# Token mixes beside the first chunks, and channel mixes at the full height of the array

## The chip, the cores and the metric

The kernel runs on one core of a Trainium2 chip. The metric is the device time of one execution in microseconds (us). The engines are called TensorE (PE in the profile; PEld is its weight load), VectorE (DVE), ScalarE (ACT), GpSimd (POOL) and SyncE (SP, which here only issues DMAs); a q behind a name is the engine's sequencer. In this kernel matmuls write to banks of PSUM, and all other tiles on the chip lie in SBUF. The record marks each run as fast or slow; all runs quoted are fast.

## The reference, cut to what matters

```python
# x: 8 x 4224 x 192, weight: 8 heads x 7 taps
w   = softmax(weight)                                  # per head
x   = causal 7-tap convolution of x along seq with w   # "conv"
theta = x @ w_theta                                    # 192 x 192, a channel mix
zr, zi = x * cos(theta), x * sin(theta)
y   = einsum('ts,bsd->btd', w_tok_r, zr) + einsum('ts,bsd->btd', w_tok_i, zi)   # 4224 x 4224 each
u   = x + y
out = u + relu(u @ w_ch)                               # a second channel mix
```

The token mixes are nearly all of the arithmetic: 33 row blocks of 128 tokens, 33 chunks of 128 source tokens, two matrices, and 1536 columns (batch times channel) in three PSUM banks of 512. That is 33 x 33 x 2 x 3 = 6534 matmuls of 128x512.

## The kernel before

The 33 chunks are handled in three passes of 11. In a pass, every row block is mixed with the pass's 11 chunks; part sums go to DRAM between the passes. The chunks of the next pass are prepared beside the mixes of this one. Only the first 11 chunks have no such company: the start has to make them while nothing, or little, can be mixed.

```python
def channel_mix(dst, tT, w):            # 192 channels = 128 + 64 rows of the array
    R = D - P                           # 64
    for q in range(2):
        v = [dst[k][:, q * D : (q + 1) * D] for k in range(2)]
        for k in range(2):              # two matmuls on all 128 rows
            pe(nc.tensor.matmul(v[k], lhsT=tT[:, 3 * q + 2 * k, :], rhs=w[:, 2 * k, :],
                                start=True, stop=False))
        for k in range(2):              # two on 64 rows each, upper and lower half
            pe(nc.tensor.matmul(v[k], lhsT=tT[k * R : (k + 1) * R, 3 * q + 1, :],
                                rhs=w[k * R : (k + 1) * R, 1, :], start=False, stop=True))

# class Chunk ... (cut)
    # conv(hp): matmuls into a PSUM bank, then ScalarE copies it to xz (two buffers);
    #           when xz is whole, four DMAs write it to the scratch xs in DRAM
    # transpose(g), theta(g): six PE transposes; channel mix; clamp on VectorE; two Sin on ScalarE
    # times_x(): z *= x on VectorE, 128x768, one for zr and one for zi

# the start: 5 PSUM banks for mixes, 3 for the rest
    y0 = [bank("y", "y") for _ in range(NP)]        # row block 0, three column blocks
    y1 = [bank("y", "y") for _ in range(2)]         # row block 1, two of three
    for i in range(nc0 + 3):
        # ... weights and chunk loads cut
        for half in range(2):
            if old: old.theta(half)                 # chunk i - 1
            next(m, 0)                              # one of five mixes per step
            if ch:
                ch.conv(2 * half); ch.conv(2 * half + 1)    # chunk i
            if old: old.times_x()
            next(m, 0)
        # ...
        for half in range(2):
            if ch: ch.transpose(half)
            next(m, 0)
```

## Time and profile before

1673.58 us, median of 4 runs (1673.18 to 1674.23).

The page of the kernel before: busy time of the engines, and the chain of work that ended last, by engine and then by line.

```profile
PE 1618.1 (97%) x8738; PEld 759.3 (45%) x8910; DVE 870.9 (52%) x1550; ACT 231.0 (14%) x366; POOL 509.7 (31%) x948
PE 93%; issue 1%; ACT 1%; DVE 1%; DMA 1%; SPq 0%; DVEq 0%; ACTq 0%
```

TensorE is the limit, but "97% busy" doesn't say how densely it works. The timeline does. These are lines of the third pass (start, length, engine, operation, count); ends overlap, so read the starts.

```profile
1294.24 0.38 PE L331 MATMUL y<-zr,wt_10762 128*128 128x512 bf16 x1
1294.46 0.38 PE L331 MATMUL y<-zi,wt_10828 128*128 128x512 bf16 x1
1294.67 0.33 PE L276 MATMUL v<-wch,uT 128*128 128x192 bf16 x2
1294.93 0.26 PE L281 MATMUL v<-wch,uT 64*128 64x192 bf16 x2
1295.12 0.34 PE L276 MATMUL v<-wch,uT 128*128 128x192 bf16 x2
1295.39 0.26 PE L281 MATMUL v<-wch,uT 64*128 64x192 bf16 x2
```

A mix starts every 0.2157 us. Two full-height channel matmuls start 82 to 94 ns apart (in the records of single instructions), two half-height ones 3 ns apart, that is, together; but each change of height takes 179 to 186 ns. All eight take 0.91 us. In the same way six transposes take 0.335 us and eight conv matmuls 0.55.

From these paces comes the measure used below. For each of TensorE's weight loads, of which no record is missing, add up what all matmuls issued before it take at the dense pace (idle matmuls, which the change adds, count as nothing). The clock minus that sum is what TensorE has **lost so far**. Before, the dense sum is 6534 x 0.2157 + 132 x 0.335 + 66 x 0.55 + 132 x 0.91 = 1610 us; of the span of 1671.0 us, 61.0 are lost: 12.2 when the first conv starts, 52.2 by 150 us, and only 8.8 in all the rest.

What it waited for (the waits view of the kernel before: who, for whom, us in total, times, longest; "..." marks lines left out, here and below):

```profile
PE pc L202 <- DMA xw<-in_x_dram: 12.2, 1, 12.2
PE th L276 <- ACT xz L209: 10.5, 6, 3.1
...
PE y L331 <- DVE wt_327 L319: 3.1, 1, 3.1
```

and one such wait in the chain of the kernel before (start, length, what):

```profile
57.51 3.02 DMA xs<-xz
60.52 0.01 issue
60.53 0.83 ACT zi L245
61.36 0.38 ACT xz L209
61.74 0.04 issue
61.78 0.24 PE th L276
```

The chain names the DMA that writes xz to scratch, and the prediction took from it that ScalarE's next copy waits for this DMA, since xz has two buffers. ScalarE's two longest sums in the waits view (to 130 us), and its timeline:

```profile
ACT xz L209 <- PE pc L202: 33.1, 15, 8.3
ACT zr L242 <- DVE ang L237: 23.5, 10, 4.9
```

```profile
59.69 0.94 ACT L242 ACTIVATE zr<-ang,half_pi 128x768 bf16<-128x768 f32 x1 [1.91 <-DVE ang L237]
60.53 0.83 ACT L245 ACTIVATE zi<-ang 128x768 bf16<-128x768 f32 x1
61.27 0.85 ACT L209 ACTIVATE xz<-pc 128x384 bf16<-128x384 f32 x2
```

The DMA in the chain writes the *other* buffer of xz. The one that the copy at 61.27 fills had been written to scratch by 53.83 us; for chunks 2 to 10 that write landed at least 4.3 us before the copy. What the copy stands behind is ScalarE's own pair of Sin (zr, zi), which waited for VectorE's clamp; in all six of TensorE's waits of this kind the copy follows the pair without a gap. So the buffers of xz are not what held the chunks here; ScalarE's order is.

The sums by stretch of the kernel before (window, its length, then busy us and count of PE, PEld, DVE, ACT and POOL, granted clock, DMA share, which passes 1 where the packets' times overlap, GB/s):

```profile
20.00:60.00 40.00, 30.16 (x202) 14.03 (x206) 26.56 (x52) 19.72 (x33) 21.28 (x39) 0.91 0.98 150
60.00:100.00 40.00, 31.40 (x268) 14.91 (x271) 26.02 (x52) 26.51 (x44) 13.76 (x24) 1.00 0.91 148
```

The clock of 0.91 leaves something out: the trace's first clock record is at 40.3 us, and until then matmuls run at half pace (transposes start 106 to 107 ns apart, and 56 later; mixes about 400 ns, and 216 later).

### The profile page before, as it was taken

Reading aid. Unit: us, or ns where it says so; the run is one execution under the profiler, and the core shown is the slowest. Engines: PE = TensorE matmul, PEld = TensorE weight load, DVE = VectorE, ACT = ScalarE, POOL = GpSimd, SP = SyncE. Lnnn points to the kernel's source line nnn. Section 1 sums busy time; section 2 is a strip of 40 time slices with the busy share of each in tenths; the row PEclk is TensorE's granted clock in tenths of the full one; section 3 lists DMA queues with packets and bytes.
Section 4 is the critical chain, followed back from the end, with each engine's and each line's share of the span. In section 5 each row is a group of like instructions: output and inputs, shape, how many; then the busy total and the mean of one; then the engine's idle time right before and its main releaser. Section 6 shows DMA issues by size and latency. Waiting matters only on the chain.

```text
span 1671.0 us, 22525 instructions
## 1 busy us (share of the span) xinstructions
PE 1618.1 (97%) x8738; PEld 759.3 (45%) x8910; DVE 870.9 (52%) x1550; ACT 231.0 (14%) x366; POOL 509.7 (31%) x948
## 2 busy tenths in 40 slices
PE   4889999999999999999999999999999999999998
PEld 2334444444444444444444444444444444444444
DVE  5664444444444434444444444446666666666664
ACT  3640111111111001111111111101111111111111
POOL 6523333333333333333332332232222222222220
PEclk9999999999999999999999999999999999999999
DMA  9957665656566677777777776776766676667661
GB/s 145 153 109 134 126 128 108 129 120 113 119 120 107 144 175 174 164 178 161 164 177 170 161 180 166 160 172 150 169 153 165 157 162 162 160 163 163 160 160 64
DMA packets 221291, 248.36 MB, mean 149 GB/s; under 512 B 58752, under 2 KB 193920, under 8 KB 221184
## 3 DMA queue, kind: packets, MB, share of 16 engines
q0 software_dynamic: 152256, 85.24, 41.7%
q1 hardware_dynamic: 68928, 161.67, 27.0%
q8 instruction: 70, 1.15, 0.3%
q14 instruction: 37, 0.30, 0.1%
HBM read 235.27 MB, written 90.83 MB: 195 GB/s over the span
## 4 chain that ended last, share of the span: by engine, by line
PE 93%; issue 1%; ACT 1%; DVE 1%; DMA 1%; SPq 0%; DVEq 0%; ACTq 0%
PE y L331 84%; PE tp L260 2%; PE v L276 2%; PE v L281 1%; PE th L276 1%; PE pc L202 1%; PE th L281 1%; DMA xs<-xz 1%; ACT xz L209 0%; ACT zi L245 0%; DVE ang L237 0%; DVE uT L264 0%; SPq L220 0%; DVE zi L251 0%; DVE pv L362 0%
## 5 line engine op out<-in xcount | busy, mean ns | idle before, releaser
L305 POOL DMA_DIRECT2D st<-in_moe_w_tok_i_dram x396 | 212.7, 544 | 682.0 <-DVE wt_1340 L319 29.6
L305 POOL DMA_DIRECT2D st<-in_moe_w_tok_r_dram x396 | 212.7, 544 | 363.4 <-issue 18.1
L364 DVE TENSOR_TENSOR pv<-y,pv 128x512 f32<-128x512 f32 x198 | 136.6, 690 | 258.6 <-PE y L331 249.3
L362 DVE COPY pv<-y 128x512 f32<-128x512 f32 x99 | 68.2, 690 | 198.8 <-PE y L331 195.3
L264 DVE COPY uT<-tp 128x768 bf16<-128x768 bf16 x132 | 73.4, 557 | 170.0 <-PE tp L260 169.6
L242 ACT ACTIVATE zr<-ang,half_pi 128x768 bf16<-128x768 f32 x66 | 61.7, 935 | 623.6 <-DVE ang L237 623.5
L368 ACT ACTIVATE ub<-pv 128x512 bf16<-128x512 f32 x99 | 62.3, 629 | 517.4 <-DVE pv L364 517.4
L237 DVE TENSOR_SCALAR ang<-th 128x384 f32<-128x384 f32 x132 | 67.5, 551 | 78.9 <-PE th L281 78.9
L386 DVE SCALAR_TENSOR_TENSOR pv<-v,pv 128x384 f32<-128x384 f32 x132 | 67.5, 553 | 75.3 <-PE v L281 75.3
L209 ACT ACTIVATE xz<-pc 128x384 bf16<-128x384 f32 x132 | 57.7, 487 | 285.0 <-PE pc L202 169.2
L187 POOL DMA_DIRECT2D xw<-in_x_dram x132 | 76.7, 592 | 66.4 <-PE pc L202 55.3
L354 DVE TENSOR_TENSOR pv<-pv,xr 128x512 f32<-128x512 f32 x99 | 66.3, 670 | 0.0
L276 PEld LDWEIGHTS <-uT 128*128 128x128 bf16 x528 | 40.2, 98 | 43.8 <-DVE uT L264 2.1
L276 PE MATMUL th<-wth,uT 128*128 128x192 bf16 x264 | 47.2, 259 | 10.7 <-ACT xz L209 10.5
L245 ACT ACTIVATE zi<-ang 128x768 bf16<-128x768 f32 x66 | 54.7, 829 | 0.0
L202 PE MATMUL pc<-xw,bands 96*64 96x192 bf16 x528 | 38.5, 264 | 15.2 <-DMA xw<-in_x_dram 12.2
L281 PEld LDWEIGHTS <-uT 64*128 64x128 bf16 x528 | 25.4, 93 | 54.9 <-issue 54.9
L276 PE MATMUL v<-wch,uT 128*128 128x192 bf16 x264 | 44.1, 249 | 0.7 <-DVE uT L264 0.7
L202 PEld LDWEIGHTS <-bands 96*64 96x64 bf16 x528 | 22.2, 113 | 44.5 <-issue 31.4
L251 DVE TENSOR_TENSOR zr<-xz,zr 128x768 bf16<-128x768 bf16 x66 | 35.0, 530 | 9.1 <-ACT zr L242 9.0
L260 PE MATMUL tp<-ident,xz 128*128 128x128 bf16 x396 | 37.5, 233 | 2.1 <-ACT xz L209 1.8
L260 PEld LDWEIGHTS <-xz 128*128 128x128 bf16 x396 | 29.6, 105 | 21.0 <-ACT xz L209 8.3
(629 smaller groups left out, 3612.4 us busy)
## 6 DMA issues: line engine op xcount, KB each, us to landing
st<-in_moe_w_tok_r_dram POOLq DMA_DIRECT2D x396, 88.0 KB, 3.3
st<-in_moe_w_tok_i_dram POOLq DMA_DIRECT2D x396, 88.0 KB, 3.3
part_83<-pv SPq DMA_DIRECT2D x33, 768.0 KB, 3.9
pv<-part_83 SPq DMA_DIRECT2D x33, 768.0 KB, 4.3
part_84<-pv SPq DMA_DIRECT2D x33, 768.0 KB, 3.8
pv<-part_84 SPq DMA_DIRECT2D x33, 768.0 KB, 5.0
out_dram<-pv SPq DMA_DIRECT2D x66, 384.0 KB, 4.0
xs<-xz SPq DMA_DIRECT2D x132, 96.0 KB, 3.7
```

What stands on the lines that cost most here:

```text
L187: nc.gpsimd.dma_start(out=self.xw[lo : lo + n, h, :, :], in_=x[:, t0 : t0 + n, :].rearrange("b s d -> s b d"),)
L202: pe(nc.tensor.matmul(pc[half * 2 * Q : (half + 1) * 2 * Q, hh * B * G : (hh + 1) * B * G], lhsT=bands[:, h, :, :].rearrange("p a m -> p ( ...
L237: dve(nc.vector.tensor_scalar(out=every_other(ang[:, :, :], k), in0=pair(th[k]), scalar1=-CLAMP, scalar2=CLAMP, op0=ALU.max, op1=ALU.min,))
L260: pe(nc.tensor.transpose(tp[:, k * P : (k + 1) * P], u[:, k * P : (k + 1) * P], ident))
L264: dve(nc.vector.tensor_copy(out=uT[:, :, :].rearrange("p k s -> p (k s)"), in_=tp[:, 0 : 6 * P]))
L276: pe(nc.tensor.matmul(v[k], lhsT=tT[:, 3 * q + 2 * k, :], rhs=w[:, 2 * k, :], start=True, stop=False,))
L305: nc.gpsimd.dma_start(out=st[a * Q : (a + 1) * Q, :, 0 : self.ncs * Q], in_=w[self.tb * P : (self.tb + 1) * P, t0 : t0 + self.ncs * Q] .re ...
L331: pe(nc.tensor.matmul(y, lhsT=w.wt[m][:, c, :, :].rearrange("p bt i -> p (bt i)"), rhs=zs[c][m][:, cols], start=(c == 0 and m == 0), stop= ...
L354: dve(nc.vector.tensor_tensor(out=self.pv[:, cols], in0=self.pv[:, cols], in1=self.xr[:, cols], op=ALU.add,))
L362: dve(nc.vector.tensor_copy(out=pj, in_=y))
L364: dve(nc.vector.tensor_tensor(out=pj, in0=y, in1=pj, op=ALU.add))
L386: dve(nc.vector.scalar_tensor_tensor(out=pk, in0=pair(v[k]), scalar=0.0, in1=pk, op0=ALU.max, op1=ALU.add,))
```

## The change

The intent: fill TensorE's waits in the start with the mixes of four row blocks instead of five thirds; take the height changes out of the channel mixes, by padding the 64-row weights with zeros to 128 rows. The diff, cut to its core (... marks cuts; the comments sum up what is cut):

```diff
-        t = constp.tile([P, 3, D], BF16, name=name)
+        t = constp.tile([P, 4, D], BF16, name=name)
+        nc.vector.memset(t[:, 1:3, :], 0.0)
 ...
-            channel_mix(th, self.xT[g], wth)     # full, full, half, half
+    def channel_mix(tT, k, w):
+        v = bank("mm", "v")
+        for b in range(2):
+            for i in range(2):
                 pe(nc.tensor.matmul(
+                    v[:, b * D : (b + 1) * D], lhsT=tT[:, 3 * k + b + i, :],
+                    rhs=w[:, 2 * b + i, :], start=(i == 0), stop=(i == 1),
                 ))
 ...
-                self.xz = wk.tile([P, B, D], BF16, name="xz", tag="xz")
+                self.xz = wk.tile([P, B, D], BF16, name="xz",
+                    tag="xw" if early[0] and self.c % 2 else "xz")
 ...
+    def times_x(self, g):                      # one step later than before
+            for z in (self.zr, self.zi): ...
+                if early[0] and z is self.zi and g == 0:
+                    nc.gpsimd.tensor_tensor(**args)
+                else:
+                    dve(nc.vector.tensor_tensor(**args))
 ...
+    class Piece:                               # one column block of one row block: 12 of them
+        def leave(self):                       # its PSUM bank is wanted
+            self.give(True)
+            if self.part is None:              # first part sum: ScalarE copies it to SBUF
+                tag = ("zr", "zi")[len(parts) % 2]     # a buffer of the next pass's chunks
+                self.part = zpool.tile([P, PC], F32, name="part", tag=tag)
+                act(nc.scalar.activation(out=self.part, in_=self.y, func=AT.Copy))
+            else:                              # later ones: VectorE adds
+                dve(nc.vector.tensor_tensor(
+                    out=self.part, in0=self.y, in1=self.part, op=ALU.add))
+        ...
+        def fill(ready, n):                    # mix n pairs (one chunk, one piece)
+            for k in range(n):
+                held = [o for o in pieces if o.y is not None]
+                can = [o for o in held if o.can(ready)]
+                new = [o for o in pieces if o.y is None and o.can(ready)]
+                if not can and new:
+                    if len(held) == 4:
+                        max(held, key=lambda o: o.c).leave()
+                    can = new
+                if not can:
+                    return n - k
+                can[0].take()
+            return 0
 ...
+        pinned[0] = True                       # VectorE's (and ScalarE's) order is fixed from here on
+        idle(12)                               # matmuls on zeros, for the clock
+        for i in range(nc0 + 2): ...
+            # conv 0 1, two pairs, theta 0 (chunk i-1), products (chunk i-2), two pairs,
+            # conv 2 3, a weight transpose, two pairs, theta 1, four Sin, two pairs,
+            # then twice: transpose, weight transpose, one pair.
+            # Where there is no pair yet and i < 5, an idle matmul.
```

The first x load is also issued before the masks are made, and the conv bands are built from one block instead of two.

## The prediction

> **What bounds the kernel.** TensorE. The page gives PE 97% of the 1671.0 us span and the chain of waits puts 93% on PE, 84% on the token mixes. In the timeline a mix matmul (128x512) follows the last every 0.2157 us, a group of six transposes takes 0.335, eight conv matmuls 0.55, eight channel-mix matmuls 0.91. Times the counts (6534 mixes, 132 transpose groups, 66 conv groups, 132 channel mixes) this is 1409.7 + 44.2 + 36.3 + 120.1 = 1610 us, an estimate from these durations. So 61 us of the span are not dense TensorE work: comparing running sum and clock, 12.2 us before the first conv (which waits for the first x load), about 40 us between 12 and 120 us, 2.2 us from 120 to 1666, and 6.6 us in the tail. The waits view names the middle part: TensorE's theta matmuls wait for ScalarE's conv evictions, and the chain goes back to the scratch write of xz (3.0 to 4.3 us each), since xz has only two buffers; chunks then come every 7 to 8 us and only five mixes share that time.
>
> **Change 1, full-height channel mixes.** The timeline of single instructions shows two full-height 128x192 matmuls starting 82 ns apart, two 64-row ones 3 ns apart (concurrent), but 179 to 186 ns at each switch between the heights, with the next weight load held back. The Trainium skill, "TensorEngine Tiling (Array Packing)", Key Properties, says that a mode switch drains TensorE; the trace agrees, about 100 ns beyond the 82. Eight full-height matmuls should need 8 x 0.082 = 0.66 us: 0.25 saved in each of 132, 33 us, of which 110 (28 us) lie in dense TensorE time, so on the critical path. Zero padding doubles those rows' arithmetic and costs nothing else.
>
> **Change 2, the start.** Four row blocks (132 mix pairs, 57 us) are mixed beside the first chunks instead of five thirds (24 us). Odd chunks' xz take other buffers, bands cost less DVE, the first x load is issued before the masks, and idle matmuls keep the clock up. Counting the new order with the durations above: 3.9 to 5.7 us for each of the first five steps, up to 7.4 for the later ones, 19 us of mixes left after the last: 112 us at best for 91 us of work, 21 lost. DVE gets 6 to 7 us per step, ScalarE 5 to 6; part sums add 12 ScalarE copies and some 20 DVE adds of about 0.65 us, hidden. The DMA engines, busy above 90% until 90 us already, get two more row blocks of weights; by their packet times a step with a chunk and half a row block needs near 8 us. I expect 24 to 35 us lost instead of 52, so about 24 saved.
>
> **Sum.** Dense 1577 + start 28 + drip 2 + tail 7 + hand-over 2 = 1616 us; 8 in 10: 1603 to 1634. Faster by over 2% 0.94, within 2% 0.05, slower 0.01.
>
> **What would show it.** The channel mix: starts 82 ns apart, one form 128*128, a pass-2 row block about 0.5 us shorter. The start: chunk steps of 7 to 8.5 us, the first conv near 11 us, no theta waiting on xz, the wait for DMA larger; mixes dense by 115 to 125 us.
>
> **What would make it wrong.** GpSimd, which now also does one product per chunk, stuck behind DMA issues that wait for buffers; VectorE over 8 us per step because evictions and weight transposes queue in fixed order; three PSUM banks for conv, theta and transposes stalling TensorE: 10 us a step would cost 20 more. If full-height matmuls of alternating weights take 0.1 us each, 19 us of change 1 vanish.

## The result, and the profile after

1632.28 us, median of 4 runs (1626.16 to 1636.74), against 1673.58. The ratio is 0.975, 95% interval 0.9718 to 0.9782, so faster. The prediction said 1616, with 1603 to 1634: the measured time lies inside, but just, and one of the four runs lies outside. Note the spread: 10.6 us over four runs, against 1.1 before.

The page of the kernel after:

```profile
PE 1599.9 (98%) x8962; PEld 793.8 (49%) x8962; DVE 879.6 (54%) x1543; ACT 238.1 (15%) x379; POOL 527.7 (32%) x961
PE 95%; DMA 2%; POOL 1%; DVE 1%; issue 0%; ACT 0%; SPq 0%; DVEq 0%; POOLq 0%
```

The timeline of the kernel after: a channel mix of the third pass is now one line, of one form.

```profile
1265.68 0.82 PE L243 MATMUL v<-wch,uT 128*128 128x192 bf16 x8
```

With 0.66 us for eight (the starts of the eight are 82 to 83 ns apart; the 0.82 includes the last one's end), the dense sum becomes 1577 us. From 150 us to the last weight load the kernel then loses only 2.9 us, so that pace is right. The channel mix is worth what was promised. The start isn't: TensorE has lost 45.3 us by 150 us, 6.9 less than before, where 28 were expected in the start and 2 at the hand-over to the next stage. The waits view of the kernel after:

```profile
PE y L290 <- DVE part L425: 7.7, 3, 5.1
PE spare L549 <- POOL ident masks.py:199: 6.7, 1, 6.7
PE tp L229 <- DVE ang L198: 6.5, 4, 3.6
```

ScalarE's xz is gone from it. VectorE stands in its place, with single waits of 3.6 and 5.1 us. (The line of "spare" is the idle matmuls waiting for their operand, before the first conv.) The stretches of the kernel after:

```profile
20.00:60.00 40.00, 33.83 (x298) 20.07 (x296) 35.98 (x60) 27.15 (x45) 33.71 (x51) 1.00 1.19 201
60.00:100.00 40.00, 33.06 (x245) 19.02 (x245) 33.33 (x57) 20.62 (x34) 19.88 (x28) 0.87 0.65 98
```

VectorE is busy 36 and 33 of 40 us: it has hardly any slack left. The granted clock is 0.87 in the second stretch, where the kernel before had 1.00. The wait of 3.6 us costs more than itself: TensorE loses 3.9 us in it, and 2.75 more from 61.6 to 67.7 us, while the granted clock is 0.5 (0.66 in the slice from 60 to 70 us).

The wait of 3.6 us in the timeline of the kernel after:

```profile
54.80 3.15 DVE L223 TENSOR_TENSOR zr<-xz,zr 128x768 bf16<-128x768 bf16 x2
...
55.40 1.65 POOL L221 TENSOR_TENSOR zi<-xz,zi 128x768 bf16<-128x768 bf16 x1
...
57.87 1.98 DVE L223 TENSOR_TENSOR zi<-xz,zi 128x768 bf16<-128x768 bf16 x1
...
59.33 2.01 POOL L221 TENSOR_TENSOR zi<-xz,zi 128x768 bf16<-128x768 bf16 x1
59.77 0.68 DVE L425 TENSOR_TENSOR part<-y,part 128x512 f32<-128x512 f32 x1
60.37 0.70 DVE L276 STREAM_TRANSPOSE wt<-st 128x512 bf16<-128x512 bf16 x1
61.00 0.98 DVE L198 TENSOR_SCALAR ang<-v 128x384 f32<-128x384 f32 x2
...
61.56 0.80 PE L229 MATMUL tp<-ident,xz 128*128 128x128 bf16 x6 [3.62 <-DVE ang L198]
```

A product on VectorE takes 0.55 us elsewhere. Here two together take 3.15 and one takes 1.98, each time with a product of GpSimd near. Behind them, in VectorE's fixed order, stand an addition of a part sum and a weight transpose, and only then the clamp that frees the PSUM bank TensorE needs. Six of VectorE's products are long like this, 9.7 us in excess of 0.55 each; the kernel before has none. A third wait, of 2.3 us before 107.11, has no long product in it: VectorE is doing clamps, three products of 0.55 us and three additions there.

### The profile page after: what moved, and what is told of

Read it like the earlier page. It is cut to its first block, busy times and chain, and to the rows that moved or that the text cites. A ratio compares the mean times of both kernels' runs of the same rounds, so it can differ in the third digit from the quotient of the medians. Undisturbed runs are those within 1.5% of the kernel's fastest.

```text
span 1630.4 us, 22878 instructions
## 1 busy us (share of the span) xinstructions
PE 1599.9 (98%) x8962; PEld 793.8 (49%) x8962; DVE 879.6 (54%) x1543; ACT 238.1 (15%) x379; POOL 527.7 (32%) x961
## 4 chain that ended last, share of the span: by engine, by line
PE 95%; DMA 2%; POOL 1%; DVE 1%; issue 0%; ACT 0%; SPq 0%; DVEq 0%; POOLq 0%
PE y L290 86%; PE v L243 5%; PE tp L229 3%; PE pc L165 1%; DMA xw<-in_x_dram 1%; POOL xw L147 1%; DMA st<-in_moe_w_tok_i_dram 1%; DVE zi L223 0%; DMA xw<-xw 0%; DVE zr L223 0%; POOL st L262 0%; DVE part L425 0%; POOL zi L221 0%; DVE ang L198 0%; DVE wt L276 0%
## 5 line engine op out<-in xcount | busy, mean ns | idle before, releaser
L290 PE MATMUL y<-zr,wt 128*128 128x512 bf16 x3267 | 1240.4, 380 | 8.4 <-DVE part L425 7.7
L290 PE MATMUL y<-zi,wt 128*128 128x512 bf16 x3267 | 1239.8, 379 | 0.0
L290 PEld LDWEIGHTS <-wt 128*128 128x128 bf16 x6534 | 628.5, 98 | 718.0 <-issue 11.7
L276 DVE STREAM_TRANSPOSE wt<-st 128x512 bf16<-128x512 bf16 (+1 forms) x594 | 366.8, 645 | 0.0
L321 DVE COPY pv<-y 128x512 f32<-128x512 f32 x87 | 60.1, 690 | 201.8 <-PE y L290 186.0
L243 PEld LDWEIGHTS <-uT 128*128 128x128 bf16 x1056 | 92.1, 99 | 34.3 <-issue 3.1
L198 DVE TENSOR_SCALAR ang<-v 128x384 f32<-128x384 f32 x132 | 67.3, 549 | 50.7 <-PE v L243 44.4
L243 PE MATMUL v<-wth,uT 128*128 128x192 bf16 x528 | 56.4, 250 | 1.1 <-DVE uT L233 0.9
L243 PE MATMUL v<-wch,uT 128*128 128x192 bf16 x528 | 54.4, 246 | 0.7 <-DVE uT L233 0.7
L229 PE MATMUL tp<-ident,xz 128*128 128x128 bf16 x396 | 33.2, 220 | 6.6 <-DVE ang L198 6.5
```

The lines of the kernel that those rows point to most:

```text
L198: dve(nc.vector.tensor_scalar(out=af[:, k * 2 * D : (k + 1) * 2 * D], in0=channel_mix(self.xT[g], k, wth), scalar1=-CLAMP, scalar2=CLAMP, ...
L229: pe(nc.tensor.transpose(tp[:, k * P : (k + 1) * P], u[:, k * P : (k + 1) * P], ident))
L243: pe(nc.tensor.matmul(v[:, b * D : (b + 1) * D], lhsT=tT[:, 3 * k + b + i, :], rhs=w[:, 2 * b + i, :], start=(i == 0), stop=(i == 1),))
L276: dve(nc.vector.transpose(self.wt[m][:, c:ce, :, :], self.st[m][:, :, c * Q : ce * Q].rearrange("p bt (c j) -> p c bt j", j=Q),))
L290: pe(nc.tensor.matmul(y, lhsT=w.wt[m][:, c, :, :].rearrange("p bt i -> p (bt i)"), rhs=zs[c][m][:, cols], start=(c == first and m == 0), s ...
```

## The experiments

Three theories for the 15 us or so by which the start falls short (45.3 lost against 28 and 2):

- **Theory 1**: GpSimd's product and VectorE's products exclude each other. The Trainium skill, "SBUF — State Buffer", section "SBUF: two separate sides", says that VectorE's second port pair is shared with GpSimd under "an exclusive lock, not a bandwidth split", for a VectorE operation with two SBUF inputs against a GpSimd operation that reads SBUF.
- **Theory 2**: VectorE simply has too much to do, in a fixed order: 22 additions of part sums, weight transposes, clamps.
- **Theory 3**: GpSimd's queue. Its product stands behind weight loads, which wait for staging buffers.

| run | us, median | TensorE's loss by 150 us | long products on VectorE, excess us |
|---|---|---|---|
| before | 1673.6 | 52.2 | 0 |
| after | 1632.3 | 45.3 | 6, 9.7 |
| e1, only the full-height channel mixes | 1645.5 | 59.0 | 0 |
| e2, after, all products on VectorE | 1623.9 | 34.9 | 0 |
| e3, after, two products on GpSimd | 1627.4 | 39.5 | 8, 11.2 |
| e4, after, least mixed piece first | 1618.1 | 31.1 | 4, 6.8 |
| e6, after, four staging buffers | 1624.4 | 38.7 | 2, 2.7 |
| e5, e2 and e4 together | 1614.9 | 27.9 | 0 |
| e7, e5 without idle matmuls | 1614.9 | 27.8 | 0 |
| e8, e5 with two xz buffers | 1645.7 | 58.9 | 0 |
| e9, e5 with two row blocks | 1627.2 | 39.4 | 0 |
| e10, e7 with four side banks | 1618.9 | 31.2 | 0 |
| e11, e5 and a useless GpSimd product | 1625.0 | 39.7 | 10, 15.0 |
| e12, e5 and GpSimd memsets | 1615.1 | 29.0 | 0 |

"Long" is over 0.7 us; the last two columns come from each run's trace, the last from its single instructions. All results were correct. The runs are from five sets of rounds; the kernel before took 1673.6 to 1674.0 us in each, so they can be compared.

**e1: the channel mixes alone.** In the kernel before, with the weights padded as in the change (not shown):

```diff
-        for q in range(2):
-            # full, full, half, half
+        for k in range(2):
+            for q in range(2):
+                for i in range(2):
+                    pe(nc.tensor.matmul(dst[k][:, q * D : (q + 1) * D],
+                        lhsT=tT[:, 3 * q + k + i, :], rhs=w[:, 2 * k + i, :],
+                        start=(i == 0), stop=(i == 1)))
```

> The kernel before with only the full-height channel mixes (same loop of chunks, same buffers). From the durations: 132 channel mixes go from 0.91 to 0.66 us, 33 us in all, of which the 110 after the start (28 us) lie in dense TensorE time and the 22 of the start are partly hidden behind waits. Expected 1643 to 1648 us. If the start's rearrangement were what paid, this would give under 15 us.

1645.45 us, against 1673.92 in the same rounds: 28.5 us. The dense sum falls by 33, and the start gives 6.8 back (59.0 lost instead of 52.2), because there TensorE only waits longer. The rest of the change is therefore worth 1645.5 - 1632.3 = 13.2 us, not the 24 (plus those few) that I had put on it.

**e2: no product on GpSimd.**

```diff
-                if early[0] and z is self.zi and g == 0:
-                    nc.gpsimd.tensor_tensor(**args)
-                else:
-                    dve(nc.vector.tensor_tensor(**args))
+                dve(nc.vector.tensor_tensor(**args))
```

> The kernel after with all four products of a chunk on VectorE, none on GpSimd. Theory 1 (the GpSimd product and VectorE's two-input products exclude each other: VectorE products of 1.2 to 2.7 us where GpSimd's is near, 0.55 elsewhere): no VectorE product over 0.7 us, TensorE's waits of 3.6 and 5.1 us in the start gone, 1617 to 1625 us. Theory 2 (VectorE has too much work in fixed order: evictions of part sums, weight transposes): 11 more products of 0.55 us, so the same time or up to 6 us slower. Theory 3 (GpSimd's queue: the product waits behind weight loads that wait for staging buffers): also faster, as theory 1.

1623.94 us, 8.3 less, though VectorE has 11 products more; no product is long. Theory 2 alone would have made it no faster. Theories 1 and 3 stand.

**e3: two products on GpSimd.**

```diff
-                if early[0] and z is self.zi and g == 0:
+                if early[0] and z is self.zi:
```

> The kernel after with both zi products of a chunk on GpSimd (two instead of one). Theory 1: more meetings, more VectorE products over 1 us (10 or more against 6), the time longer by 5 us or more. Theory 2: VectorE has 6 us less work in the start, so faster by some us.

1627.43 us (1626.16 to 1628.84): not slower, and by the medians 4.9 faster, though the runs of the two overlap. The long products were 8 and their excess 11.2 us, only 1.5 more than after, while VectorE was spared 11 products, 6 us. Theory 1's forecast of the time failed, and theory 2 has a share. It looks as if VectorE's time as a whole is what is short, whether it goes into products, into being held, or into additions.

**e4: fewer additions.** The list of pieces that can be mixed is in the order of row blocks, so the early ones come back for one chunk each time, and each visit costs an addition.

```diff
-                    can = new
+                    can = [min(new, key=lambda o: o.c)]
```

> The kernel after, but a free PSUM bank goes to the piece with the fewest chunks mixed, instead of the first in the list: by counting the order, 10 VectorE additions of part sums instead of 22, 2 instead of 17 of them before the last chunk. GpSimd's product is kept. Theory 2: 10 us of VectorE work out of the start, the waits of TensorE for VectorE mostly gone, about 10 us faster. Theory 1: the long products stay, and only the waits for additions go: 2 to 5 us faster.

1618.05 us (1615.56 to 1624.95), 14.2 less: more than either forecast. VectorE has 10 additions instead of 22 (6.6 us instead of 14.6). Four long products are left, with 6.8 us in excess instead of 9.7, so the gain is not from the additions alone.

**e5: both cures.**

> All products on VectorE and, for a free bank, the piece with the fewest chunks mixed. If the two costs (long products beside GpSimd's, 22 part-sum additions on VectorE) are separate, TensorE loses about 28 us by 150 us from the start, against 45.3 in the kernel after, 34.9 without the GpSimd product and 31.1 with the other order alone: 1611 to 1616 us. If they are one and the same slack, no better than 1617.

1614.87 us (1614.79 to 1615.40 in five runs). The loss by 150 us is 27.9, as expected; the spread has shrunk to 0.6 us. The two cures overlap: 8.3 and 14.2 us apart, 17.4 together. The stretches of this run:

```profile
20.00:60.00 40.00, 36.55 (x326) 21.95 (x325) 36.94 (x74) 29.36 (x49) 26.79 (x49) 1.00 1.24 208
60.00:100.00 40.00, 40.00 (x305) 22.61 (x303) 28.57 (x58) 26.20 (x42) 15.72 (x28) 1.00 0.89 148
```

From 60 to 100 us TensorE is busy without a break at full clock, with VectorE at 28.6 of 40. From 20 to 60 VectorE is still busy 36.9 of 40 us.

**e6: GpSimd's queue.**

```diff
-            st = wpool.tile([P, NQ, NCMAX * Q], BF16, name="st", tag="st", bufs=3)
+            st = wpool.tile([P, NQ, NCMAX * Q], BF16, name="st", tag="st", bufs=4)
```

> The kernel after with four staging buffers for raw token weights instead of three, so that GpSimd's queue, in which the product stands behind weight loads, no longer waits for a VectorE transpose. Theory 3 (the queue makes the product late): the waits of 3.6 and 5.1 us go, 1620 to 1625 us. Theories 1 and 2: the products still meet, VectorE still does the additions; 1628 to 1636 us.

1624.43 us, 7.9 less: what theory 3 expected. But the trace shows how: with an earlier queue the products meet less often (2 long ones, 2.7 us excess). The queue sets *when* GpSimd's product runs; e6 doesn't say what the meeting itself costs. For that, e11 and e12.

**e11 and e12: the meeting by itself.** All results come from VectorE, as in e5. GpSimd does something useless when VectorE's first product of a step is done:

```diff
                 dve(nc.vector.tensor_tensor(**args))
+                if early[0] and z is self.zi and g == 0:
+                    # e11
+                    nc.gpsimd.tensor_tensor(out=scratch[0], in0=self.xf[:, cols],
+                                            in1=self.zr[:, cols], op=ALU.mult)
+                    # e12, in its place
+                    nc.gpsimd.tensor_copy(out=scratch[0][:, 0:8],
+                                          in_=self.zr[:, cols.start : cols.start + 8])
+                    nc.gpsimd.memset(scratch[0], 0.0)
+                    nc.gpsimd.memset(scratch[0], 1.0)
```

> Both cures, all results from VectorE, and in each step one useless GpSimd product of the same size (128x768, two inputs in SBUF) that starts when VectorE's first product is done, its result never read. Theory 1: VectorE's products right after it last 1.2 us or more in most of the 11 steps, with no other change of VectorE's work; 3 to 10 us slower than the 1614.9 without it. If the long products came from something else in the kernel after (order, queue): all products stay at 0.55 us and the time within 1 us.

> The same with two GpSimd memsets of that tile behind an 8-element copy, instead of the product: GpSimd is busy at the same place, but hardly reads SBUF. Theory 1 in the form that a read port is shared (the Trainium skill's page on SBUF says so): VectorE's products stay at 0.55 us, the time within 1 us of 1614.9. If any GpSimd work beside VectorE costs: long products here too.

e11 took 1624.98 us (1620.61 to 1626.50), 10.1 more than e5; e12 took 1615.05, 0.2 more. The groups of e11 from 0 to 112 us (busy us, mean ns of one):

```profile
L221 DVE TENSOR_TENSOR zr<-xz,zr 128x768 bf16<-128x768 bf16 x22 | 23.9, 1087 | 0.1
...
L223 POOL TENSOR_TENSOR scratch<-xz,zr 128x768 bf16<-128x768 bf16 x11 | 19.0, 1729 | 19.6 <-DVE zr L221 19.6
...
L221 DVE TENSOR_TENSOR zi<-xz,zi 128x768 bf16<-128x768 bf16 x22 | 15.2, 692 | 0.0
```

and the same groups of e12:

```profile
L221 DVE TENSOR_TENSOR zi<-xz,zi 128x768 bf16<-128x768 bf16 x22 | 12.1, 549 | 0.2 <-ACT zi L213 0.2
L221 DVE TENSOR_TENSOR zr<-xz,zr 128x768 bf16<-128x768 bf16 x22 | 12.1, 548 | 0.1
...
L227 POOL MEMSET scratch<- 128x768 bf16 x11 | 8.4, 759 | 0.0
```

One of the 11 meetings in the timeline of e11:

```profile
50.23 0.55 DVE L221 TENSOR_TENSOR zi<-xz,zi 128x768 bf16<-128x768 bf16 x1
...
50.48 1.79 POOL L223 TENSOR_TENSOR scratch<-xz,zr 128x768 bf16<-128x768 bf16 x1 [4.36 <-DVE zr L221]
50.69 1.99 DVE L221 TENSOR_TENSOR zr<-xz,zr 128x768 bf16<-128x768 bf16 x1
...
52.61 0.55 DVE L221 TENSOR_TENSOR zi<-xz,zi 128x768 bf16<-128x768 bf16 x1
```

GpSimd's product begins at 50.48 and ends at 52.27. VectorE's, begun at 50.69, ends at 52.68: 0.4 us after it, as if it had waited for the whole of it; all ten long ones end 0.41 to 0.43 us after the GpSimd product beside them. Their excess is 15.0 us in all. A GpSimd that is as busy (19.9 us against 19.0), but hardly reads, changes nothing: in e12 the records of single instructions have six memsets that overlap a product, by 0.14 to 0.55 us, and those products take 0.545 to 0.557 us. Nor is it GpSimd's issuing of DMAs: in e5, 32 of the 44 products overlap an issue, and none takes more than 0.56 us. That a GpSimd product with SBUF inputs blocks VectorE's two-input product is shown; that the read port is what they share is the skill's account, and e12 agrees with it, as far as its short overlaps go.

**e7: the idle matmuls.**

```diff
-        idle(12)
-                if i < 5:
-                    idle(few)
```

> The run with both cures, without the idle matmuls (12 before the first conv, about 40 in the first five steps). If they keep the granted clock up: some stretches at half clock before 50 us, 2 to 6 us slower than with them. If they only stand in the way of the real matmuls: 1 to 4 us faster.

1614.91 us against 1614.87: no difference. The granted clock is 0.72 and 0.76 in the slices from 20 to 30 and from 30 to 40 us, 1.00 with the idle matmuls; TensorE isn't the limit there, so nothing is lost by it.

**e8: two buffers of xz.**

```diff
-                    tag="xw" if early[0] and self.c % 2 else "xz",
+                    tag="xz",
```

> The run with both cures, but every chunk's xz in the same two buffers, as in the kernel before. If the scratch write of xz was what held the chunks up before: ScalarE's copies wait for it again in most steps from the fourth on, up to 1.5 us each, 4 to 10 us slower. If the longer steps (7.4 us of TensorE work against 5) hide the write: within 2 us.

1645.66 us (1644.63 to 1652.12), 30.8 more; the largest effect of all, and not for the reason I gave. The timeline of e8:

```profile
81.14 0.55 DVE L220 TENSOR_TENSOR zr<-xz,zr 128x768 bf16<-128x768 bf16 x1
81.61 0.55 DVE L220 TENSOR_TENSOR zi<-xz,zi 128x768 bf16<-128x768 bf16 x1
...
82.24 1.64 ACT L172 ACTIVATE xz<-pc 128x384 bf16<-128x384 f32 x4 [4.96 <-issue]
82.78 0.36 PE L165 MATMUL pc<-xw,bands 96*64 96x192 bf16 x4 [1.94 <-ACT xz L172]
```

The last product that reads the old xz ends at 82.16, and ScalarE's copy into that buffer starts 0.08 us later; for each of chunks 2 to 10 it is 0.08 to 0.16 us. It isn't the DMA to scratch that holds the buffer in this order, it is the products: the change does them one step later than before, so it *needs* more buffers of xz. The scratch write of the old xz had landed at least 6.5 us before each of these copies, so it would not have held them.

**e9: two row blocks.**

```diff
-    EARLY = 4
+    EARLY = 2
```

> The run with both cures, with two row blocks mixed beside the first chunks instead of four. Of 57 us of early mixes 28.5 are left. If the number of row blocks fills the waits of the later steps: TensorE runs dry in steps 6 to 12, 8 to 16 us slower than with four (1623 to 1631 us). If the other parts of the change (more xz buffers, orders) already keep the steps short, since a step then needs only about 6 us: within 4 us.

1627.17 us, 12.3 more, in the expected range. Up to 80 us the loss is almost that of e5 (29.8 against 26.9); after it TensorE runs dry (37.8 against 26.8 at 100 us). The four row blocks earn their keep in the second half of the start.

**e10: the bank of the idle matmuls.**

```diff
-        open_psum(stack, 5, 3)
+        open_psum(stack, 4, 4)
```

> Both cures, no idle matmuls, and the PSUM bank that those used given to conv, theta and transposes: four banks for them, four for mixes. In the first five steps TensorE's transposes wait 0.76 us in each of two steps for a clamp to free one of three banks. If those three banks set the pace of the early steps (6.9 us each, for 3.1 us of work): 2 to 5 us faster, 1610 to 1613. If ScalarE's and VectorE's chain of fixed order does: the same within 1 us.

1618.91 us, 4.0 more than e7, which neither reading expected. By 40 us the loss is lower (23.3 against 24.6), so the three banks seem to cost a little (one trace of each); but the waits of this run show what the fifth mix bank was for:

```profile
PE y L287 <- ACT part L420: 3.7, 5, 0.9
PE y L287 <- DVE part L422: 2.1, 3, 0.9
```

Four pieces are held at most, and the fifth bank lets the next begin while one is still being emptied.

## Why the prediction was right or wrong

- **What bounds it**: right, TensorE's dense work and its losses in the start; the loss view holds in all runs with the same paces. But the cause that it gave for those losses, the scratch write of xz, was a misreading of the chain: that write had landed at least 4.3 us before each copy, and the copies stood behind ScalarE's Sin pair.
- **Channel mixes, 33 us of dense work, 28 of them on the critical path**: right. e1 measured 28.5. The Trainium skill, "TensorEngine Tiling (Array Packing)", Key Properties, says that a mode switch drains TensorE; the trace has about 100 ns more for each switch (179 to 186 against 82).
- **The start, 28 lost (24 to 35) and 2 for the hand-over**: wrong; 45.3. This is the term that failed. The step was "part sums add 12 ScalarE copies and some 20 DVE adds of about 0.65 us, hidden", together with "DVE gets 6 to 7 us per step", which I compared with TensorE's 7.4 and found smaller. They are not hidden: with a margin of 0.4 to 1.4 us a step, in a fixed order, the additions (22, 14.6 us) and the long products (9.7 us in excess) push VectorE past TensorE, and TensorE waits for clamps and additions, then runs at a lower clock. e4 got 14.2 us back by removing additions (and with them two of the long products), e2 8.3 by removing the GpSimd product, e5 17.4 with both, at 27.9 lost.
- **The listed risk, GpSimd's product behind its DMA issues**: right that it would hurt, but only half the reason. e6 shows the queue matters (7.9 us); e11 shows that the product also blocks VectorE by itself (10.1 us). I had counted it as help for VectorE.
- **DMA, "a step needs near 8 us"**: wrong. e5 moves 208 GB/s from 20 to 60 us, with steps of about 7 us, and its waits view lists no wait of TensorE for a DMA in the first 150 us. Packet times overlap; their sum isn't a floor.
- **First conv near 11 us**: wrong; 12.4, against 12.2 before. With x loaded earlier, TensorE waits there for VectorE's bands (1.4 us in the waits view).
- **First steps 3.9 to 5.7 us by TensorE's count**: too short but for the very first; the next four take 6.2 to 7.1 in e5. VectorE, busy 36.9 of 40 us in e5, goes with that pace; neither the idle matmuls (e7) nor the three side banks alone (e10) set it. What exactly would shorten these steps was not tried further.
- **Buffers of xz**: I took the extra buffers for relief from the scratch write. e8 shows that in this order they are a condition for the rest, since the products come a step later. What took the theta waits away may be that the Sin now follow the copies; that order was not tried alone.

So the first part was right in mechanism and size. Of the second, the filling pays (e9), but the step "hidden" failed and the size was off: 28 to 30 us lost were expected, 45.3 measured, and 27.9 reached once VectorE had room. That the total still fell inside the range owes something to its width of 31 us, twice the miss in that term. That e5 lands on 28 is partly luck: the early steps of that count were too short, and the cause that it gave for the waits was not the one in the trace. The version of e5, two small edits away from the change, is the fastest found: 1614.87 us, ratio 0.9646 to the kernel before (0.9633 to 0.9659).

## What to carry to other kernels

When a limit is filled up, cost the second-busiest engine step by step with everything the filling brings (here the additions for part sums), because here a margin of about a microsecond a step, in a fixed order, was none: a part sum kept in SBUF cost VectorE 0.68 us for each 128x512 addition, 1.6 times the 0.43 us of the pair of mix matmuls that it may serve. Choose the work that comes back to a buffer so that each visit is long: one line that took the least mixed piece first saved 14 us. Moving an elementwise operation to GpSimd may cost VectorE more than it saves if both read SBUF with two inputs at the same moment (none on GpSimd 1623.9 us, one 1632.3, two 1627.4): look for instructions that are longer than their group's usual length. And when a chain of waits names a DMA, check with the waiting engine's own records that the DMA belongs to the buffer in question.

## What the Trainium skill lacked or had wrong

- "SBUF — State Buffer" ("SBUF: two separate sides"): confirmed by e11, where a 128x768 VectorE product of 0.55 us took 2.0 to 2.3 us beside a GpSimd product. But "starts first" doesn't fit every case: in the kernel after, a VectorE product recorded from 57.87 to 59.85 us was held while GpSimd was issuing DMAs, before GpSimd's own product is recorded (59.33), and ended before it. GpSimd's recorded times are rough, so this is left open.
- "GPSIMD Engine Reference" ("Engine selection") puts two-input elementwise work on GpSimd at about 2 times VectorE's time. Here a bf16 product of 128x768 took 1.65 us undisturbed against 0.55, that is 3 times; the pair that the page measured is in fp32.
- "TensorEngine Tiling (Array Packing)" (Key Properties) says that a mode switch drains TensorE but gives no number. Here, between full and half height: 179 to 186 ns from start to start, against 82 to 94 within full height; eight matmuls at mixed heights 0.91 us, at full height with zero padding 0.66.
- "TensorE: Matmul & The Clock Gate" ("Why this matters for your kernels") advises to keep TensorE from idling for long. A wait of 3.6 us indeed left a granted clock of 0.66 in the slice after it; but idle matmuls kept for that purpose gained nothing in these first steps, where TensorE was not the limit (e7, 1614.91 against 1614.87 us).
